# A new order of instructions at the start and at the end of a fused attention and mixture kernel, and half a weight unit loaded early

## The chip, the cores and the metric

The kernel runs on one core of a Trainium2 chip. The metric is the device time of one execution in microseconds (us). The core has five engines with a queue of instructions each: TensorE (PE in the rows; its weight loads are PEld), VectorE (DVE), ScalarE (ACT), GpSimd (POOL) and SyncE (SP), which in this kernel issues all transfers. An engine works through its own queue strictly in order; between engines, semaphores hold an instruction back until its inputs are there and the buffer that it writes is free.

## What is computed

Three layers follow one another on 4608 rows of 512 numbers:

```python
# attention without a score matrix: 8 batches, 8 heads, 576 positions, 64 wide
q_s = softmax(q, over the 64);  k_s = softmax(k, over the 576 positions)
x   = q_s @ (k_s.T @ v)                       # per batch and head -> x [4608, 512]
# feed-forward with a cosine gate (w_in, w_out are given as float64)
h = x @ w_in;  g = h * cos(h);  x2 = g @ w_out          # 2048 wide, back to 512
# soft mixture: 32 slots, 8 experts of 4 slots each
logits = x2 @ phi;  d = softmax(logits, over rows);  c = softmax(logits, over slots)
slot_in = d.T @ x2;  slot_out[e] = relu(slot_in[e] @ w1[e]) @ w2[e]
out = c @ slot_out
```

## The kernel before

The rows are worked in nine blocks of 512. The last block is cut into two parts of 256, so there are ten parts. A part has 16 steps, one for each 128 of the 2048 columns of `w_in`; the kernel numbers the steps through, from 0 to 159, and the last 32 have half the width.

One step is this chain. TensorE makes `h` for 128 columns by 12 matmuls (`mm1`, L906): x and `w_in` are each split into a high and a low part, and three products are summed. The result stands in one of three PSUM buffers ("h"). `round_u` (L925) rounds it to a whole number of turns, on ScalarE or VectorE as a table says; `frac` (L934, VectorE) takes the fraction; `cosine` (L940, ScalarE) looks up a sine; `gate` (L943, VectorE) multiplies and writes `g` into the big buffer G. The gate frees the PSUM buffer, so `mm1` of step s waits for the gate of step s-3. Every two or four steps `logits` (L946) adds those steps to the slot logits, in the PSUM bank LT, and `g_tr` (L963, VectorE) transposes their `g` in place. After the 16 steps of a part come the softmax sums: `p1` copies the logits out of PSUM, `p2` transposes them for the combine weights (`c1` to `c3`), `p3` takes the running maximum, `p4` the exponentials, `p5`, `copies` and `take_copy` spread them out, `g_mm` (L1099) adds d.T @ g to four PSUM banks, and `g_add` (L1114) moves these into an accumulator.

The rounded number and the fraction stand in a tile T of four places of 512 (`tbuf`, L357); step s uses place s modulo 4.

The start is special. Before step 0 the first block's x is made: `k_max`, `k_sub`, `k_exp` (the softmax of k), `k_v` (k_s.T @ v on TensorE), `k_fin`, `q_max` to `q_mul` (the softmax of q), `q_tr` and `q_tr_ev` (transposes and their copies), `q_kv` (TensorE), and the split of x by `x_hi` (ScalarE) and `x_lo` (VectorE). At the same time the float64 weights arrive in eight chunks each of `w_in` and `w_out` and are turned into float32 by VectorE, ScalarE and GpSimd (`convert`, L763, three instructions a piece; `conv_wi` parts 3 and 4, L805, split a piece into high and low). The `w_out` pieces are written back to DRAM for the end, and with phi they are folded into one matrix for the logits (`w2_tr`, `w2_tr_ev`, `w2_mm`, `w2_sum`). Step f needs piece f of `w_in`, so steps 0 to 15 run while pieces still arrive; blocks 1 and 2 are prepared in the same time. `warm` matmuls (L1691) compute nothing: they fill TensorE while it waits.

The end is special too. After step 159 follow the sums of the last part, `fold`, `gT`, `si` (the slot inputs, with `w_out`), `siT`, and the experts: `w1` (16 matmul groups), `hs`, `hT`, `w2` (17 groups), `so`, `sx`, and then `om` and `oe`, which multiply and copy out nine blocks, and `out`, which stores them. The experts' weights are 32 MB. They come in units of 1 MB through SyncE's queue (`load_unit`, L1188), each into a buffer that the earlier work no longer needs (`slots`, L1164); `units_after` (L1746) says what each waits for. Unit 20, the first of `w2`, goes to T, and waits for the last gate.

What sets the order: one list of work items is written out by the kernel. `PLACES["AT"]` gives every item a number, items are issued in the order of their numbers, and each engine's queue is that list cut down to the engine. `PLACES["ENG"]` gives the engine of items that can go to two or three (D is VectorE, A ScalarE, P GpSimd).

Of the kernel before, what the change touches and what calls it, by code (L numbers as in the profile page):

```python
# [17 lines left out]
AX = mybir.AxisListType  # L18
# [10 lines left out]
                "warm": [95, 30, 116, 83, 20, 16, 26, 18, 63, 10, 138, 33, 40, 120, 27, 2, 12, 6,  # L29
# [5 lines left out]
                "k_max": [17, 19, 21, 23, 25, 29, 32, 39, 173, 177, 195, 222, 178, 223, 229, 236,  # L35
# [3 lines left out]
        "k_tr": [44, 242],  # L39
        "k_dg": [46, 50, 247, 262],  # L40
        "k_bc": [53, 280],
        "k_bc_ev": [65, 281, 528, 642, 834, 949, 1107, 1272],
                "k_sub": [66, 88, 96, 69, 323, 338, 326, 335, 542, 541, 529, 531, 654, 648, 661,
            643, 837, 861, 841, 844, 970, 951, 958, 950, 1125, 1121, 1111, 1116, 1281, 1285, 1274,
            1278],
                "k_exp": [75, 93, 101, 77, 356, 347, 543, 532, 662, 672, 869, 875, 992, 1001, 1151,
            1166, 1306, 1313],
                "k_v": [102, 107, 362, 363, 556, 558, 679, 684, 885, 888, 1013, 1019, 1188, 1193,
            1358, 1365],
        "k_fin": [115, 381, 574, 697, 895, 1028, 1205, 1375],  # L50
# [232 lines left out]
def attention_cosine_moe_softmoe(  # L283
# [35 lines left out]
    def misc():  # L319
        return pst("m", 4)  # L320
# [1555 lines left out]
```

## Time and profile before

| | us |
|---|---|
| three timed runs, median (lowest, highest) | 656.82 (655.79, 657.02) |
| the profiled execution's own time | 659.79 |
| its span, from the first to the last instruction | 657.8 |
| TensorE busy in the span | 625.2 (95%) |
| VectorE busy | 536.6 (82%) |
| ScalarE busy | 366.3 (56%) |
| GpSimd busy | 128.4 (20%) |
| first big matmul of step 0 | 33.36 |
| last part's `g_mm` ends, near | 583.2 |

The span is the profiled execution's; its own time stands 2.0 us over the span, and 3.0 us over the median of the timed runs. A row of the timeline is read so: start, length, engine, line, operation, what it writes and reads, how many were merged into the row, and in square brackets how long the engine had been idle before and what ended that.

### The profile page before, as it was taken

What the parts mean: (1) busy time and instruction counts of PE and PEld (TensorE: products, weight loads), DVE (VectorE), ACT (ScalarE), POOL (GpSimd) and SP (SyncE); (2) the same over time, 40 slices, a digit from 0 to 9 for tenths busy, and PEclk for the clock granted to TensorE, in tenths of its full rate; (3) what the DMA queues carried; (4) which work ended last, traced back from release to release, by engine and by line L of the source; (5) the groups of instructions that cost most, each with busy time, mean ns of one, the idle gap of its engine ahead of it and who ended that gap; (6) DMA issues with size and microseconds to landing.
All of it is one profiled execution on the core that took longest, in us unless ns stands there. A gap on an engine that the chain in (4) does not pass through costs nothing.

```text
span 657.8 us, 18204 instructions
## 1 busy us (share of the span) xinstructions
PE 625.2 (95%) x7745; PEld 474.6 (72%) x7745; DVE 536.6 (82%) x1075; ACT 366.3 (56%) x642; POOL 128.4 (20%) x131
## 2 busy tenths in 40 slices
PE   5899999999999999999999999999999999999990
PEld 4577777688868877877788788778878989843440
DVE  7889999999999988998979987879988878842251
ACT  4789988657475476457466542635536456530051
POOL 4343535243133043041220120001200000000000
PEclk9889999999999999999999999999999999999996
DMA  9997965354321442133302300021003338899968
GB/s 314 301 398 246 341 222 145 115 154 129 87 53 34 121 114 82 49 101 112 80 18 80 125 0 2 1 77 54 1 1 124 135 111 308 323 372 422 386 233 347
DMA packets 60992, 103.88 MB, mean 158 GB/s; under 512 B 9456, under 2 KB 40560, under 8 KB 55920
## 3 DMA queue, kind: packets, MB, share of 16 engines
q1 hardware_dynamic: 60912, 102.74, 46.4%
q8 instruction: 60, 0.98, 0.6%
q14 instruction: 20, 0.16, 0.1%
HBM read 88.15 MB, written 14.57 MB: 156 GB/s over the span
## 4 chain that ended last, share of the span: by engine, by line
PE 74%; DMA 9%; ACT 7%; DVE 6%; issue 1%; POOL 1%; SPq 0%; DVEq 0%; POOLq 0%; ACTq 0%
PE ps_h L920 53%; PE ps_m L1107 6%; PE ps_LT L958 5%; DMA w_u<-in_moe_w_dram 3%; PE ps_m L708 2%; PE ps_m L523 2%; DMA Q<-in_q_dram 2%; DMA out_dram<-ob 1%; DMA G<-in_moe_w_out_dram 1%; PE ps_h L1312 1%; DMA wo<-G 1%; ACT T L928 1%; ACT T L941 1%; PE ps_LT L1696 1%; ACT G L775 1%
## 5 line engine op out<-in xcount | busy, mean ns | idle before, releaser
L920 PE MATMUL ps_h<-XH,W 128*128 128x512 f32 x1024 | 328.7, 396 | 0.9 <-DVE G L944 0.9
L920 PEld LDWEIGHTS ps_h<-XH,W 128*128 128x128 f32 x1024 | 193.3, 189 | 53.5 <-issue 8.1
L920 PE MATMUL ps_h<-XL,W 128*128 128x512 f32 x512 | 200.5, 392 | 0.0
L941 ACT ACTIVATE T<-T 128x512 f32<-128x512 f32 (+1 forms) x160 | 92.6, 587 | 93.8 <-DVE T L936 93.5
L928 ACT ACTIVATE T<-ps_h,quarter 128x512 int32<-128x512 f32 (+1 forms) x123 | 79.4, 646 | 80.1 <-PE ps_h L920 79.2
L944 DVE TENSOR_TENSOR G<-T,ps_h 128x512 f32<-128x512 f32 (+1 forms) x160 | 99.4, 624 | 25.0 <-ACT T L941 19.6
L920 PEld LDWEIGHTS ps_h<-XL,W 128*128 128x128 f32 x512 | 96.8, 189 | 18.8
L936 DVE SCALAR_TENSOR_TENSOR T<-T,ps_h 128x512 f32<-128x512 int32 (+1 forms) x160 | 99.0, 623 | 10.2 <-ACT T L928 8.9
L965 DVE STREAM_TRANSPOSE G<-G 128x512 f32<-128x512 f32 (+1 forms) x160 | 98.4, 637 | 0.3 <-PE ps_LT L958 0.2
L420 POOL TENSOR_TENSOR Q<-Q,qm 128x512 f32<-128x512 f32 x33 | 35.2, 1083 | 150.3 <-DVE qm L417 104.6
L920 PE MATMUL ps_h<-xe,W 128*128 128x256 f32 x384 | 48.0, 285 | 0.0
L920 PEld LDWEIGHTS ps_h<-xe,W 128*128 128x128 f32 x384 | 46.6, 192 | 1.6 <-DVE G L944 0.8
L684 POOL TENSOR_TENSOR KVB<-KVB,km 128x576 f32<-128x576 f32 x22 | 33.1, 1526 | 72.9 <-DVE km L677 50.6
L441 POOL TENSOR_TENSOR Q<-Q,qm 128x512 f32<-128x512 f32 x27 | 27.9, 1060 | 81.6 <-DVE qm L434 64.1
L958 PE MATMUL ps_LT<-G,wphi 128*32 128x128 f32 (+1 forms) x1280 | 38.9, 265 | 1.0 <-issue 1.0
L958 PEld LDWEIGHTS ps_LT<-G,wphi 128*32 128x32 f32 x1280 | 30.3, 110 | 9.3 <-issue 6.6
L1107 PE MATMUL ps_m<-G,A 32*32 32x512 f32 x1024 | 35.7, 598 | 0.0
L941 ACT ACT_TABLE_LOAD x24 | 30.8, 1283 | 0.4
L930 DVE TENSOR_SCALAR T<-ps_h 128x512 int32<-128x512 f32 (+1 forms) x37 | 22.8, 615 | 7.0 <-PE ps_h L920 7.0
L1107 PEld LDWEIGHTS ps_m<-G,A 32*32 32x32 f32 x1024 | 16.9, 103 | 13.4 <-issue 7.9
L417 DVE TENSOR_REDUCE qm<-Q 128x8 f32<-128x512 f32 x36 | 24.1, 673 | 2.7 <-DMA Q<-in_q_dram 2.7
L1125 DVE SCALAR_TENSOR_TENSOR gacc<-gacc,ac,ps_m 128x512 f32<-128x512 f32 x32 | 23.2, 733 | 2.3 <-PE ps_m L1107 2.3
(214 smaller groups left out, 716.9 us busy)
## 6 DMA issues: line engine op xcount, KB each, us to landing
w_u<-in_moe_w_dram SPq DMA_DIRECT2D x22, 1024.0 KB, 8.0
KVB<-in_k_dram SPq DMA_DIRECT2D x16, 576.0 KB, 5.2
KVB<-in_v_dram SPq DMA_DIRECT2D x32, 256.0 KB, 4.4
out_dram<-ob SPq DMA_DIRECT2D x8, 1024.0 KB, 9.1
rwi<-in_moe_w_in_dram SPq DMA_DIRECT2D x7, 1024.0 KB, 10.2
G<-in_moe_w_dram SPq DMA_DIRECT2D x7, 1024.0 KB, 7.8
rwo<-in_moe_w_out_dram SPq DMA_DIRECT2D x5, 1024.0 KB, 11.0
wo<-G SPq DMA_DIRECT2D x16, 256.0 KB, 6.0
```

Of the source, the lines that this page charges most:

```text
L417: nc.vector.reduce_max(out=qm[:, t], in_=qv(t), axis=AX.X)
L420: (nc.vector if eng == "DVE" else nc.gpsimd).tensor_tensor(out=qv(t), in0=qv(t), in1=qm[:, t].unsqueeze(2).to_broadcast([128, 8, 64]), op= ...
L441: (nc.vector if eng == "DVE" else nc.gpsimd).tensor_tensor(out=qv(t), in0=qv(t), in1=qs[:, t].unsqueeze(2).to_broadcast([128, 8, 64]), op= ...
L684: (nc.vector if eng == "DVE" else nc.gpsimd).tensor_tensor(out=k_t[:, t], in0=k_t[:, t], in1=km[:, t].unsqueeze(1).to_broadcast([128, KC, ...
L920: nc.tensor.matmul(out=u_t[s], lhsT=w[:, wi, kk, o:o + 128], rhs=x[xi][:, kk], start=(kk == 0 and n == 0), stop=(kk == 3 and n == 2),)
L928: nc.scalar.activation(out=t.bitcast(I32), in_=u_t[s], func=ACTF.Identity, bias=quarter)
L936: nc.vector.scalar_tensor_tensor(out=t, in0=t.bitcast(I32), scalar=0.25, in1=u_t[s], op0=ALU.subtract, op1=ALU.subtract)
L941: nc.scalar.activation(out=t_t[s], in_=t_t[s], func=ACTF.Sin, scale=-UNDER_TWO_PI)
L944: nc.vector.tensor_tensor(out=g_of(s), in0=t_t.pop(s), in1=u_t.pop(s), op=ALU.mult)
L958: nc.tensor.matmul(out=lt_t[d][32 * c:32 * c + 32, 0:w], lhsT=w2sb[:, f], rhs=g[:, w * c:w * c + w], start=(f0 == 0), stop=(f0 == NF - 1),)
L965: nc.vector.transpose(out=g_of(s), in_=g_of(s))
L1107: nc.tensor.matmul(out=st["gp"][i][32 * c:32 * c + 32].rearrange("p (f b) -> p f b", f=NF) if d < NB else st["gp"][i][32 * c:32 * c + 32]. ...
```

## The change

1. The numbers in `AT` are new for the items up to about step 20 (and those issued among them) and for those after step 127. Between them the list is the same, item for item. SyncE's queue has the same transfers in the same order, with one more (point 3), which stands between units 5 and 6.
2. 24 letters of `ENG` change up to step 40. Net of exchanges they move three `k_sub` from VectorE to GpSimd; `cD` (the low part of a `w_in` piece) of pieces 1, 5, 7 and 8 from VectorE to GpSimd and of piece 15 the other way; one `q_mul` from GpSimd to VectorE; three `w2_tr_ev` and four `round_u` from ScalarE to VectorE. In the last two parts four more `round_u` change, from VectorE to ScalarE.
3. T becomes two tiles, T and T2, of two places each. The last two parts use T alone (four places of 256). T2 is free after the gates of steps 126 and 127, and half of unit 20 is loaded into it then (`load_half`); the other half still goes to T, after the last gate.
4. In the last two parts one `g_tr` transposes two steps' `g` (512 columns) in place of two instructions of 256.
5. The logits of the last two parts: `p2` and `c1` to `c3` of both are issued after `si`; `p3` and `p4` of the last part read the logits from PSUM and no longer wait for the copy of `p1`. The `fill` matmuls (they compute nothing) stand elsewhere.

```diff
-        "k_sub": "DDDPPDDDPPDPPPPPPPDPPPPDPPPPPPDP",
+        "k_sub": "DPDDDPPPPPPPPPPPPPDPPPPDPPPPPPDP",
-        "cD": "DDPPPDPDDPPPPPPP",
+        "cD": "DPPPPPPPPPPPPPPD",
...
-        t = t_t[s] = tbuf[:, s % 4, 0:parts[s // NF][2]]
+        if s < 16 * (NB - 1):
+            t = t_t[s] = tb[s % 4 // 2][:, s % 2]
+        else:
+            t = t_t[s] = tb[0][:, s % 4 // 2, 256 * (s % 2):256 * (s % 2) + 256]
...
+        if d >= NB - 1:
+            f = tile_of(d, f)
+            x = gs(d)[:, f:f + 2] if d < NB else gs(d)[:, f // 8, f % 8:f % 8 + 2]
+            x = x.rearrange("p a t -> p (a t)")
+        nc.vector.transpose(out=x, in_=x)
...
-        nc.vector.reduce_max(out=es, in_=st["lt"], axis=AX.X)
+        nc.vector.reduce_max(out=es, in_=lt_of(d), axis=AX.X)
...
+    def lt_of(d):
+        return st["lt", d] if d < NB else lt_t[d][:, 0:parts[d][2] // 4]
...
+    def load_half():
+        ut["T2"] = sbt([128, 2, 512], "T2", name="w2_h")
+        nc.sync.dma_start(out=ut["T2"], in_=w2_src(units[slots.index("T")])[:, 2:4])
...
+            if slots[i] == "T":
+                ut[un], src = (t, ut.pop("T2")), src[:, 0:2]
...
+    op(("half",), DMA, 1.3, load_half, more=2.3, slack=1.4, after=[("g", S8 - 1), ("g", S8 - 2)])
```

VectorE at the start, before: from the reciprocal of the first q sums (L434) to the first sum of `k_fin` (L716). L684 is `k_sub`, L448 `q_mul`, L800 the join of a converted piece, L815 `cD`.

```order
L434 RECIPROCAL qm<-qm 128x32
L800 SCALAR_TENSOR_TENSOR G<-G,rwo 128x512
L448 TENSOR_TENSOR B<-Q,qm 128x8x64 x2
L800 SCALAR_TENSOR_TENSOR A<-A,rwi 128x512
L684 TENSOR_TENSOR KVB<-KVB,km_76 128x576
L800 SCALAR_TENSOR_TENSOR A<-A,rwi 128x512
L684 TENSOR_TENSOR KVB<-KVB,km_76 128x576
L815 TENSOR_TENSOR W_228<-A,W_228 128x4x128
L448 TENSOR_TENSOR B<-Q,qm 128x8x64
L815 TENSOR_TENSOR W_228<-A,W_228 128x4x128
L417 TENSOR_REDUCE qm<-Q 128x8
L716 TENSOR_REDUCE rs<-ps_m 128x2 x2
```

The same stretch now:

```order
L434 RECIPROCAL qm<-qm 128x32
L684 TENSOR_TENSOR KVB<-KVB,km_77 128x576
L448 TENSOR_TENSOR B<-Q,qm 128x8x64 x2
L684 TENSOR_TENSOR KVB<-KVB,km_77 128x576 x2
L800 SCALAR_TENSOR_TENSOR A<-A,rwi 128x512
L448 TENSOR_TENSOR B<-Q,qm 128x8x64 x2
L815 TENSOR_TENSOR W_266<-A,W_266 128x4x128
L716 TENSOR_REDUCE rs<-ps_m 128x2 x2
```

The subtractions for k now stand ahead of all conversions, and two conversions (one L800, one L815) have left the stretch.

ScalarE before, from the last two parts of x (L593) to the first sine (L941); L928 is the rounding of a step, L427 the exponentials of q, and L775 with A a new `w_in` piece.

```order
L593 CAST XH_97<-ps_m 128x512 x2
L775 ACTIVATE G<-rwo 128x512 x2
L813 CAST W_358<-A 128x4x128
L786 ACTIVATE rwo<-rwo,low 128x512
L928 ACTIVATE T<-ps_h,quarter 128x512
L427 ACTIVATE Q<-Q 128x512 x4
L849 COPY cst<-ps_m 128x4x128
L928 ACTIVATE T<-ps_h,quarter 128x512
L775 ACTIVATE A<-rwi 128x512
L941 ACT_TABLE_LOAD
L941 ACTIVATE T<-T 128x512
```

The same stretch now (L931 is the rounding, L944 the sine):

```order
L593 CAST XH_98<-ps_m 128x512 x2
L786 ACTIVATE rwo<-rwo,low 128x512
L775 ACTIVATE G<-rwo 128x512
L849 COPY cst<-ps_m 128x4x128
L786 ACTIVATE rwo<-rwo,low 128x512
L849 COPY cst<-ps_m 128x4x128
L813 CAST W_367<-A 128x4x128
L775 ACTIVATE G<-rwo 128x512
L427 ACTIVATE Q<-Q 128x512 x4
L931 ACTIVATE T<-ps_h,quarter 128x512
L775 ACTIVATE A<-rwi 128x512
L944 ACT_TABLE_LOAD
```

The exponentials of q stand ahead of the first rounding, and the second rounding has gone to VectorE; the new `w_in` piece still stands ahead of the table load for the first sine.

TensorE at the end, before, from the last `g_mm` (L1107) on; L1696 are fill matmuls, L1239 and L1250 `fold`, L1266 `gT`, L1282 `si`, L1298 `siT`.

```order
L1107 MATMUL ps_m<-G,KVB_u 32x512 x32
L1696 MATMUL ps_LT<-ones 128x512
L1239 MATMUL ps_h<-gacc,rf 32x256 x8
L1250 MATMUL ps_h<-G,rf 32x2x64 x16
L1266 MATMUL ps_m<-ident,gacc 128x128 x4
L1696 MATMUL ps_LT<-ones 128x512 x2
L1282 MATMUL ps_m<-KVB_u,gT 32x512 x4
L1696 MATMUL ps_LT<-ones 128x512 x2
L1077 MATMUL ps_h<-esacc,rr 128x1
L1282 MATMUL ps_m<-KVB_u,gT 32x512 x4
L1696 MATMUL ps_LT<-ones 128x512
L1282 MATMUL ps_m<-wo_u,gT 32x512 x8
```

The same stretch now (L1125 is `g_mm`, L1725 fill, L1266 and L1277 `fold`, L1293 `gT`, L1309 `si`, L1008 `p2`):

```order
L1125 MATMUL ps_m<-G,KVB_u 32x512 x32
L1725 MATMUL ps_LT<-ones 128x512
L1266 MATMUL ps_h<-gacc,rf 32x256 x8
L1277 MATMUL ps_h<-G,rf 32x2x64 x16
L1725 MATMUL ps_LT<-ones 128x512
L1293 MATMUL ps_m<-ident,gacc 128x128 x4
L1725 MATMUL ps_LT<-ones 128x512
L1095 MATMUL ps_h<-esacc,rr 128x1
L1309 MATMUL ps_m<-KVB_u,gT 32x512 x8
L1309 MATMUL ps_m<-wo_u,gT 32x512 x8
L1008 MATMUL ps_m<-ident,late 64x64 x4
```

The four `si` now follow one another; the three fills that stood between them are gone, and the small matmul for the sum (L1077, now L1095) stands ahead of them.

## Rows read from the trace of the kernel before

**Rows 1.** Windows by stage: per engine busy us (instructions), granted clock, DMA share, GB/s.

```profile
33.30:38.50 5.20, 5.20 (x16) 4.07 (x14) 4.39 (x8) 3.40 (x7) 0.66 (x1) 0.56 1.04 396
...
60.00:90.00 30.00, 29.70 (x356) 23.57 (x354) 29.65 (x56) 29.41 (x51) 12.74 (x11) 1.00 0.95 310
...
120.00:574.00 454.00, 451.76 (x5642) 364.65 (x5641) 400.89 (x809) 249.34 (x429) 74.17 (x72) 1.00 0.30 91
...
627.00:658.00 31.00, 14.43 (x330) 6.12 (x326) 12.31 (x22) 10.38 (x22) 0.00 (x0) 0.80 0.76 306
```

**Rows 2.** Timeline of TensorE: first k_v, and the first matmul of step 0.

```profile
21.41 2.33 PE L708 MATMUL ps_m<-KVB 64*64 64x66 f32 x144
...
33.36 0.80 PE L920 MATMUL ps_h<-XH,W 128*128 128x512 f32 x1
```

**Rows 3.** Timeline of VectorE, ScalarE and GpSimd, 32 to 46 us.

```profile
32.15 0.69 DVE L417 TENSOR_REDUCE qm<-Q 128x8 f32<-128x512 f32 x1 [1.65 <-DMA Q<-in_q_dram]
...
38.48 0.69 ACT L928 ACTIVATE T<-ps_h,quarter 128x512 int32<-128x512 f32 x1 [1.64 <-PE ps_h L920]
...
39.44 0.66 POOL L790 TENSOR_SCALAR rwi<-rwi 128x512 int32<-128x512 uint16 x1 [5.49 <-DMA rwi<-in_moe_w_in_dram]
...
42.20 0.67 ACT L775 ACTIVATE A<-rwi 128x512 f32<-128x512 f32 x1
...
42.89 1.28 ACT L941 ACT_TABLE_LOAD   x1
...
44.19 0.63 ACT L941 ACTIVATE T<-T 128x512 f32<-128x512 f32 x1
...
44.85 0.69 DVE L944 TENSOR_TENSOR G<-T,ps_h 128x512 f32<-128x512 f32 x1 [0.37 <-ACT T L941]
```

**Rows 4.** Timeline of GpSimd and VectorE: `cD` on either, and two that overlap.

```profile
40.19 1.31 POOL L815 TENSOR_TENSOR W<-A,W 128x512 fp32r<-128x512 f32 x1
...
55.11 1.27 POOL L448 TENSOR_TENSOR B<-Q,qm 128x512 f32<-128x512 f32 x1 [0.86 <-DVE qm L434]
55.40 1.53 DVE L800 SCALAR_TENSOR_TENSOR G<-G,rwo 128x512 int32<-128x512 int32 x1
...
59.70 0.68 DVE L815 TENSOR_TENSOR W<-A,W 128x512 fp32r<-128x512 f32 x1
```

**Rows 5.** Windows, the end of the steps and the expert weights.

```profile
500.00:536.00 36.00, 36.00 (x553) 30.96 (x562) 31.37 (x71) 22.59 (x43) 0.00 (x0) 1.00 0.32 119
...
584.00:590.00 6.00, 5.73 (x71) 2.90 (x63) 1.63 (x5) 0.85 (x3) 0.00 (x0) 1.00 0.97 326
590.00:619.00 29.00, 28.79 (x332) 11.85 (x335) 7.42 (x11) 1.52 (x3) 0.00 (x0) 1.00 1.01 418
```

**Rows 6.** Timeline of SyncE: the issue of units 21 and 22.

```profile
583.31 2.94 SPq L1208 DMA_DIRECT2D G<-in_moe_w_dram  x2
```

**Rows 7.** The chain that ended last: its wait for the expert weights.

```profile
606.08 17.84 DMA w_u<-in_moe_w_dram
```

**Rows 8.** Timeline of VectorE around the last gate (L944; L965 are transposes).

```profile
575.96 0.38 DVE L944 TENSOR_TENSOR G<-T,ps_h 128x256 f32<-128x256 f32 x1
576.26 1.73 DVE L965 STREAM_TRANSPOSE G<-G 128x256 f32<-128x256 f32 x5
...
579.25 1.40 DVE L965 STREAM_TRANSPOSE G<-G 128x256 f32<-128x256 f32 x4
```

**Rows 9.** Groups by shape, 495 to 580 us: busy us, mean ns; idle.

```profile
L965 DVE STREAM_TRANSPOSE G<-G 128x512 f32<-128x512 f32 x14 | 9.5, 693 | 0.2 <-PE ps_LT L958 0.2
```

**Rows 10.** Timeline of TensorE: last `g_mm`, and fills and `si` after it.

```profile
580.85 2.35 PE L1107 MATMUL ps_m<-G,KVB_u 32*32 32x512 f32 x64
...
587.88 0.73 PE L1696 MATMUL ps_LT<-ones 128*128 128x512 f32 x2
...
589.65 0.50 PE L1696 MATMUL ps_LT<-ones 128*128 128x512 f32 x1
590.08 1.92 PE L1282 MATMUL ps_m<-wo_u,gT 128*32 128x512 f32 x16
```

More of the change, by code (lines that the diff above doesn't have):

```diff
@@ L41 @@
-        "k_bc": [53, 280],
-        "k_bc_ev": [65, 281, 528, 642, 834, 949, 1107, 1272],
-                "k_sub": [66, 88, 96, 69, 323, 338, 326, 335, 542, 541, 529, 531, 654, 648, 661,
+                "k_max": [1, 6, 7, 11, 8, 14, 16, 22, 166, 174, 179, 225, 162, 170, 176, 180, 451,
[3 rows of a table added]
+        "k_tr": [30, 230],
+        "k_dg": [36, 40, 248, 254],
+        "k_bc": [43, 274],
+        "k_bc_ev": [44, 290, 508, 642, 834, 949, 1107, 1272],
+                "k_sub": [61, 59, 69, 78, 317, 319, 335, 334, 520, 516, 527, 539, 654, 648, 661,
@@ L222 @@
+        "gT": [2075, 2076],
+        "gTe": [2080, 2082],
+        "si": [2081, 2084, 2085, 2087],
+        "siT": [2095, 2096, 2099],
[14 rows of a table added]
+        "out": [2201, 2210, 2216, 2225, 2232, 2243, 2255, 2256],
+        "half": [1792],
     },
     "ENG": {
-        "k_sub": "DDDPPDDDPPDPPPPPPPDPPPPDPPPPPPDP",
+        "k_sub": "DPDDDPPPPPPPPPPPPPDPPPPDPPPPPPDP",
         "q_sub": "PDPPPPPDPPPPPPPPPPPPPPPPPPPPPPPPPDPP",
-        "q_mul": "DDDPDPPPPPPPPPPPPPPPPPDPPPPPPPPPPPPP",
+        "q_mul": "DDDDPPPDPPPPPPPPPPPPPPDPPPPPPPPPPPPP",
@@ L356, in attention_cosine_moe_softmoe @@
     bbuf = sbt([128, 4, 512], "B")
-    tbuf = sbt([128, 4, 512], "T")
+    tb = [sbt([128, 2, 512], tag) for tag in ("T", "T2")]
     kv_t = [abuf[:, 0, 256 * i:256 * i + 256].rearrange("p (h t d) -> p h t d", h=2, t=2)
@@ L978, in p1 @@
     def p1(d):
-        st["lt"] = sbt([128, 128], "LTs")[:, 0:parts[d][2] // 4]
-        nc.scalar.copy(out=st["lt"], in_=lt_t.pop(d)[:, 0:parts[d][2] // 4])
+        w = parts[d][2] // 4
+        if d < NB - 1:
+            st["lt", d] = sbt([128, 128], "LTs")
+        elif d == NB - 1:
+            late = sbt([128, 128], "phi", name="late")
+            st["lt", d], st["lt", d + 1] = late[:, 0:w], late[:, w:2 * w]
+        nc.scalar.copy(out=st["lt", d], in_=lt_t[d][:, 0:w])
+    def lt_of(d):
+        return st["lt", d] if d < NB else lt_t[d][:, 0:parts[d][2] // 4]
     def p2(d):
-        pm = st["t"] = misc()
+        pm = st["t", d] = misc()
         if d < 8:
-            nc.tensor.matmul(out=pm[:, 0:128], lhsT=st["lt"], rhs=ident, start=True, stop=True)
+            nc.tensor.matmul(out=pm[:, 0:128], lhsT=st["lt", d], rhs=ident, start=True, stop=True)
             return
@@ L991, in p2 @@
                 out=pm[64 * h:64 * h + 64, 0:64].rearrange("p (e s) -> p e s", e=2),
-                lhsT=st["lt"], rhs=cols[:, h], start=True, stop=True,
+                lhsT=st["lt", d], rhs=cols[:, h], start=True, stop=True,
             )
     def p3(d):
-        nc.vector.reduce_max(out=es, in_=st["lt"], axis=AX.X)
+        nc.vector.reduce_max(out=es, in_=lt_of(d), axis=AX.X)
         if d == 0:
@@ L1351, in e_w2 @@
             return
+        w = ut["w2", eg, u]
         for x in range(2):
             for q4 in range(4):
+                wq = w[q4 // 2][:, q4 % 2] if isinstance(w, tuple) else w[:, q4]
                 nc.tensor.matmul(
@@ L1643, in step_ops @@
                + [past("warm", i) for i in range(NWARM)] * (d == 0 and f == n - 1))
-            for i in range(s - n + 1, s + 1):
-                op(("tr", i), DVE, cost(0.05, 0.56), g_tr, i, after=[("tl", s)])
+            for i in range(s - n + 1, s + 1, 1 if nt == 512 else 2):
+                op(("tr", i), DVE, 0.61, g_tr, i, after=[("tl", s)])
     def tls(d):
@@ L1655, in post_ops @@
         op(("p1", d), ACT, 0.25 if big else 0.2, p1, d,
-           after=[("tl", 16 * d + 15), past("p2", d - 1), past("p4", d - 1)])
+           after=[("tl", 16 * d + 15), past("p2", d - 1) if d < NB - 1 else None, past("p4", d - 1)])
         op(("p2", d), PE, 0.15 if big else 0.25, p2, d, take="m", after=[("p1", d)])
@@ L1659, in post_ops @@
         op(("p3", d), DVE, 0.42 if big else 0.36, p3, d,
-           after=[("p1", d), past("p6", d - 1), past("p4", d - 1)])
+           after=[("p1", d) if d < NB else ("tl", 16 * d + 15), past("p6", d - 1), past("p4", d - 1)])
         op(("p4", d), ACT, (0.6 if d else 0.35) if big else 0.5, p4, d, table="exp",
@@ L1675, in post_ops @@
                + each("tc", d)
-               + ([("tr", 16 * d + i) for i in range(NF)] if jq == 0 else []))
+               + ([("tr", 16 * d + i) for i in range(0, NF, 1 if big else 2)] if jq == 0 else []))
         for i in range(4):
@@ L1762, in lus @@
     def lus(*kind):
-        return [("lu", i) for i, u in enumerate(units) if u in kind]
+        return [("lu", i) for i, u in enumerate(units) if u in kind] + [("half",)] * (
+            units[slots.index("T")] in kind
+        )
+    op(("half",), DMA, 1.3, load_half, more=2.3, slack=1.4, after=[("g", S8 - 1), ("g", S8 - 2)])
     unit_ops(0, 23)
@@ L1769, in attention_cosine_moe_softmoe @@
     for i in range(NFILL):
-        op(("fill", i), PE, 0.26, keep_warm, 1, at=FILL, after=[("p1", D)])
+        op(("fill", i), PE, 0.26, keep_warm, 1, at=FILL, after=[("p1", D), ("p4", D)])
     for x in range(2):
```

104 lines of the change are left out of this document (49 added, 55 removed), and 162 rows, old and new, of the table PLACES.

## Prediction

> **What bounds the kernel now.** I read the windows by stage first, to see which engine has no room in which stretch. From 120 to 574 us TensorE is busy 451.8 of 454 us at full clock: what is won or lost ahead of that stretch goes through it unchanged, since one list of work runs there without gaps. From 60 to 90 us TensorE has 29.70 of 30 us, but VectorE 29.65 and ScalarE 29.41 too, so three engines bound this stretch at once and GpSimd, with 12.74 us, is the only one with room. From 33.3 to 38.5 us TensorE works at a granted clock of 0.56, the lower level. From 627 us on TensorE has 14.4 of 31 us; the chain of small products, multiplications and stores there is not touched by the change, so it is a tail of fixed length [rows 1].
>
> Then I read the timelines of single engines at the two places where the list is new. At the start, the reader is to see what the first gates wait for: step 0's matmuls begin at 33.36 [rows 2], its rounding at 38.48, its gate only at 44.85 [rows 3]. At the end, the windows and the chain that ended last show that not TensorE but the transfer of the expert weights decides: 418 GB/s and a DMA share of 1.01 from 590 to 619 us [rows 5], and 17.84 us of the chain from 606.08 on are a wait for a transfer [rows 7]. So the time is the start's delay, plus a dense middle, plus the arrival of the last weight unit, plus the tail. The change acts on the first and the third.
>
> **The start.** Step 0's gate, which frees the first of three PSUM buffers, is at the end of a chain on ScalarE: a new `w_in` piece (42.20, 0.67 us), the load of the sine table (42.89, 1.28), the sine (44.19, 0.63), then on VectorE the gate (44.85, 0.69), done at 45.54 [rows 3]. From the start of the first to the end of the last are 3.34 us. The transfer that brings that piece had landed at 39.44, when GpSimd's part of it began [rows 3]; between 39.17, where step 0's rounding ends, and 42.20 ScalarE worked off four exponentials of q, a copy and the rounding of step 1, as the order shows. In the new order the exponentials stand ahead of step 0's rounding, one copy stands earlier and the rounding of step 1 has gone to VectorE. So the piece can begin when it lands, at 39.44, and the gate ends at 39.44 + 3.34 = 42.78 instead of 45.54: 2.76 us earlier. Step 3 waits for that gate.
>
> This holds if steps 0 to 2 are through by then. Before step 0's last matmuls stood the low part of x on VectorE, and ahead of it now the maximum of q that waits for its transfer until 32.15 and takes 0.69 us [rows 3]. With about 0.7 us for the low part and 0.8 for a matmul at the low clock (the first took that [rows 2]), step 0 ends near 34.3 instead of just under 38.48: up to 4.2 us, which is the far end of the gain. The near end: if TensorE, with fewer warm matmuls ahead, works one more step at 0.56, that costs 5.20 x (1 - 0.56) = 2.3 us [rows 1], and the 2.76 shrinks to 0.5; a second such step would make it a loss of 1.8. I take -2.5: nearly the whole 2.76, since the gate hangs on a landing and on ScalarE's own order, with 0.26 off for what follows.
>
> What follows is steps 3 to 40. Net, six pieces of work leave VectorE (three `k_sub`, three `cD`, each near the 0.68 us of a `cD` [rows 4]) and eight come (four roundings, three `w2_tr_ev`, one `q_mul`): (8 - 6) x 0.68 = 1.4 us more. ScalarE gives up seven, some 4.8 us at the 0.69 of a rounding [rows 3]. GpSimd takes six and gives one: a `cD` lasts 1.31 us there [rows 4], so 5 x 1.31 = 6.6 us, in an engine that is idle more than half of 60 to 90 [rows 1]. ScalarE's relief is worth something only where it, and not VectorE, ended a wait; VectorE's 1.4 us are hidden only where it is not full. The bounds for this part are +1.4, all of it on the path, and -0.7, one rounding less in front of the steps' sines; I take +0.26, near nothing, because four of the six subtractions and conversions that move stand ahead of step 0, where VectorE still waits for transfers (1.65 us before 32.15 alone [rows 3]).
>
> **The end of the steps.** In the last two parts an instruction on 512 columns takes 693 ns [rows 9] and two on 256 take 2 x 0.346 = 0.69 (1.73 for five [rows 8]): the joined transposes save nothing by themselves. They stand otherwise among the gates, so the last gate (ended 576.34 [rows 8]) may come 0.35 to 0.7 us later, and half a unit's transfer with it. After it, `p3` no longer waits for a copy, and the transposes that followed (four, 1.40 us, from 579.25 [rows 8]) are spread; I put the last `g_mm`, which began its final run at 580.85 [rows 10], at 0.2 us earlier.
>
> Half of unit 20, 0.524 MB, leaves the full stretch: at 418 GB/s that is 1.25 us [rows 5]. It is loaded from about 517 us on instead, in a stretch where the DMA share is 0.32 [rows 5]; there it costs nothing. Behind it the queue has a second loss: units 21 and 22 were issued at 583.31 only, when G is free [rows 6], and from 584 to 590 the transfers moved 326 GB/s instead of 418, that is 6 x 92 = 0.55 MB or 1.3 us too little [rows 5]. If the shorter unit 20 is through before unit 21 is issued, the 1.25 us turn into a longer pause and the gain is only the 0.2 us by which `g_mm` ends earlier; if the queue stays full, 1.25 us and up to the 1.3 us of the pause come back, -2.6 together. Both ends rest on rows of this stretch; I take -1.4, the 1.25 and the 0.2, because a share of 0.97 at 584 to 590 says that the queue still had packets under way.
>
> After `g_mm` three groups of fills that stood between the `si` (0.73 and 0.50 us are two of them, [rows 10]) leave the path, some 1.7 us of TensorE. That is not added: `w1` waits for the units anyway [rows 7]. If that cover were gone, it would count.
>
> **The sum.** -2.5 - 1.4 = -3.9. The profiled execution has a span of 657.8 and its own time is 659.79; these become 653.9 and 655.9. The median of the runs shown, 656.82, is 3.0 below that own time, so I forecast 655.9 - 3.0 = 652.9.
>
> **Rival 1: the lead is spent on VectorE.** All 1.4 us of VectorE's extra work fall on the path, one block by GpSimd of 0.85 us (below) is added, and the start is left with -2.5 + 1.4 + 0.85 = -0.25. With half of the half unit's gain, -0.6, the sum is -0.85: 656.0. For it: 29.65 of 30 [rows 1]. Against it: a lead of TensorE is lost only once, and ScalarE gains 4.8 us in the same stretch.
>
> **Rival 2, slower: GpSimd's new work holds VectorE up.** One `k_sub` or `cD` reads two operands from SBUF. When a GpSimd multiplication ran from 55.11 to 56.38, a VectorE join that began at 55.40 lasted 1.53 us, where a like instruction takes 0.68 [rows 4]: 0.85 us lost, and its end came 0.55 after GpSimd's. Five more such instructions on GpSimd, at 0.85 to a whole 1.31 us each and 1.08 in the middle, are 5.4 us in a stretch where VectorE has no reserve: -3.9 + 5.4 = +1.5, that is 658.3. It cancels the gain from 3.9 us of stalls on and is measurably slower from 5.2. Against it: some of the five stand ahead of step 0, and VectorE may be waiting where they run.
>
> The Trainium skill ("SBUF — State Buffer", Who interferes with whom) has the rule behind this rival: VectorE's second pair of ports is shared with GpSimd, and of a VectorE instruction with two SBUF inputs and a GpSimd instruction that reads SBUF the one that starts second is wholly blocked until the first ends. The row agrees within 0.13 us: 56.38 + 0.68 is 57.06, and the join ended at 56.93. By that rule each of the five costs VectorE up to its whole length where the two meet; by the reading that they only slow each other, less.
>
> **Rival 3: the half unit buys nothing.** Unit 21 stays tied to the end of `g_mm`; the end gives -0.2, the start -2.5: 654.1. For it: the issue at 583.31 right behind the last `g_mm` [rows 6, 10]. Against it: the share of 0.97.
>
> That the change does not do what it says is a rival in the start: if the pieces of `w_in` and q land later because the transfers themselves slip, nothing has reserve, since the maximum of q and the `w_in` piece stand in order ahead of everything; a slip would pass on one to one. It is inside rival 1's time.
>
> **Chances.** The forecast 0.50, rival 1 0.22, rival 3 0.14, rival 2 0.14. About 0.2%, 1.3 us, is what a measurement of this kernel can tell from no change. The forecast and rival 3 are faster, and a part of rival 1, 0.07: faster 0.71. The other 0.15 of rival 1 is within: same 0.15. Rival 2: slower 0.14. The forecast's own range is 651 to 655, from a full -1.25 - 1.3 at the end to one without it. The low end with the far start (-4.2) and the far end (-2.6) would be 650.0; I stop at 650.2. The high end, 657.6, takes in rival 1 and the near half of rival 2.
>
> **What would show it.** Step 0's gate should end near 42.8 and the `w_in` piece before the table load begin at 39.4, not later. The last gate of the steps should come 2 to 3 us earlier than 576.34. Unit 21 should be issued near 580.6, and the gap in the transfers behind it be smaller. The last wait for `w1` should end some 3.9 us earlier, and the tail from there stay at 31 us. The forecast is wrong if TensorE's granted clock in steps 0 to 2 stays low for a second step, if VectorE has several conversions of 1.3 us or more beside GpSimd's, or if the pause behind unit 20 grows by as much as the unit shrank.

## The result, and the profile after

The changed kernel takes 650.61 us (median of 4, 650.04 to 651.63) against 656.52 for the kernel before; the ratio is 0.9917, 95% interval 0.9895 to 0.9938. Measured again later (experiment 12) it is 0.9915, 0.9890 to 0.9940. That is 5.5 us of 656.6 (0.0083 x 656.6; the two medians differ by 5.9); forecast were 3.9, and 652.9 us.

Two executions have to be compared with care. The one behind [rows 1 to 10] took 659.79 us, 3.3 over its median. Experiment 1 took a second profile of the kernel before, with a span of 653.3 instead of 657.8. What differs is a transfer. Each transfer comes in sixteen parts; the table has the times at which the first, the fifteenth and the last part landed, the start of step 3, the end of the last step, and how long after it TensorE's last w2 group began and the last weight unit landed (worked out from the traces; us).

```
                    w_out chunk 1          w_in chunk 2           step 3  last step  w2     unit
before [rows]       26.06  30.15  31.07    34.85  38.53  39.37    46.01   574.33     52.17  52.13
before again        26.30  28.05  28.34    34.60  35.92  37.14    41.82   570.26     51.53  51.49
changed             26.20  27.39  28.99    34.56  36.11  36.46    39.95   565.61     51.39  50.16
changed again       26.29  27.78  29.29    34.71  36.30  36.61    40.09   566.11     51.39  50.92
start only (exp. 2) 26.18  27.59  29.22    34.63  36.34  36.52    39.99   566.76     52.16  52.12
end only (exp. 3)   26.38  27.94  28.48    34.49  36.09  36.27    41.50   569.97     51.39  50.75
no half (exp. 4)    26.32  27.91  29.21    34.68  36.53  36.60    40.08   565.74     51.71  51.66
```

In the first profile two parts of one chunk came 4 to 5 us after the first, and the landings behind them in the table and at w_in chunk 3 (48.54, against 46.35 in the second profile) were 2 to 3 us late; in none of the other thirteen profiles did a part of that chunk come 4 us late (at most 3.6). So the like-for-like gain at step 3 is 41.82 - 39.95 = 1.9 us, not the 6.1 that the two first profiles show, and at the end of the steps 570.26 - 565.61 = 4.7.

Windows of the changed kernel (us, then busy time and count of PE, PEld, DVE, ACT, POOL, granted clock, DMA share, GB/s):

```profile
12.40:17.50 5.10, 4.08 (x14) 2.96 (x12) 5.03 (x11) 4.33 (x9) 2.12 (x2) 1.00 1.17 319
17.50:21.00 3.50, 3.16 (x128) 2.88 (x131) 3.28 (x7) 3.50 (x7) 0.00 (x0) 1.00 1.08 348
...
33.30:38.50 5.20, 5.20 (x29) 3.72 (x29) 5.13 (x12) 4.31 (x7) 1.88 (x2) 1.00 1.04 405
...
60.00:90.00 30.00, 29.01 (x362) 23.10 (x361) 28.27 (x56) 27.85 (x49) 18.12 (x15) 1.00 0.93 299
...
584.00:590.00 6.00, 6.00 (x51) 1.58 (x45) 2.47 (x13) 0.52 (x2) 0.00 (x0) 1.00 1.01 423
590.00:619.00 29.00, 28.95 (x360) 12.91 (x352) 5.84 (x5) 1.90 (x4) 0.00 (x0) 1.00 0.83 342
```

The same view of the kernel before, second profile:

```profile
12.40:17.50 5.10, 0.92 (x4) 0.40 (x3) 5.03 (x9) 4.74 (x10) 2.17 (x2) 0.94 1.17 315
17.50:21.00 3.50, 2.85 (x11) 2.59 (x12) 3.50 (x7) 2.87 (x6) 0.00 (x0) 0.50 1.08 346
21.00:24.00 3.00, 3.00 (x81) 2.48 (x83) 3.00 (x6) 2.96 (x6) 1.62 (x1) 0.55 1.03 217
...
60.00:90.00 30.00, 29.42 (x380) 22.37 (x379) 29.87 (x56) 29.94 (x54) 15.98 (x14) 1.00 0.95 307
```

Before, TensorE worked 0.92 of 5.10 us from 12.4 to 17.5 and then had the lower clock until 24 us (the record has 0.5 from 16.86 to 23.69). Now twelve of the warm matmuls stand there (37 in all, as before; 20 of them began ahead of 9 us, now 8 do), and from 14.71 us on the clock is full, from 33.3 to 38.5 too, where the first profile had 0.56. One thing about this column has to be known: the changed kernel's trace has no record of the clock before 14.71 us, and where there is none the view prints 1.00. The matmuls tell what the clock was: those of 512 columns that follow one another begin 0.43 us apart until 14.70 and 0.23 apart from there on, so before 14.71 the lower of the two levels held.

At the end the window of 584 to 590 is full (423 GB/s); the pause now lies ahead of it, from 579 to 583. From 590 to 619 the transfers' share is 0.83, since the last unit has landed at 615.77, and TensorE waits for no unit there. From 60 to 90 VectorE and ScalarE are busy 1.6 and 2.1 us less ([rows 1] had 29.65 and 29.41). Of the timelines, first the changed kernel: `k_v`, the maximum of q, the `w_in` piece, table load, sine and first gate:

```profile
19.17 2.41 PE L708 MATMUL ps_m<-KVB 64*64 64x66 f32 x144 [0.21 <-ACT rwi L786]
...
30.08 0.69 DVE L417 TENSOR_REDUCE qm<-Q 128x8 f32<-128x512 f32 x1 [0.79 <-DMA Q<-in_q_dram]
...
36.55 0.68 ACT L775 ACTIVATE A<-rwi 128x512 f32<-128x512 f32 x1 [0.87 <-DMA rwi<-in_moe_w_in_dram]
37.24 1.28 ACT L944 ACT_TABLE_LOAD   x1
38.54 0.63 ACT L944 ACTIVATE T<-T 128x512 f32<-128x512 f32 x1
...
39.20 0.69 DVE L947 TENSOR_TENSOR G<-T,ps_h 128x512 f32<-128x512 f32 x1
```

The kernel before, second profile (answers to [rows 2 to 4]); ScalarE's rows from the rounding of step 0 to the `w_in` piece follow one another without a gap:

```profile
22.18 3.01 PE L708 MATMUL ps_m<-KVB 64*64 64x66 f32 x144
...
34.65 0.67 ACT L928 ACTIVATE T<-ps_h,quarter 128x512 int32<-128x512 f32 x1
35.22 2.18 ACT L427 ACTIVATE Q<-Q 128x512 f32<-128x512 f32 x4
37.31 0.57 ACT L849 COPY cst<-ps_m 128x512 f32<-128x512 f32 x1
37.77 0.69 ACT L928 ACTIVATE T<-ps_h,quarter 128x512 int32<-128x512 f32 x1
38.35 0.67 ACT L775 ACTIVATE A<-rwi 128x512 f32<-128x512 f32 x1
...
41.01 0.69 DVE L944 TENSOR_TENSOR G<-T,ps_h 128x512 f32<-128x512 f32 x1 [1.00 <-ACT T L941]
...
51.27 1.27 POOL L448 TENSOR_TENSOR B<-Q,qm 128x512 f32<-128x512 f32 x1 [0.88 <-DVE qm L434]
51.55 1.53 DVE L800 SCALAR_TENSOR_TENSOR G<-G,rwo 128x512 int32<-128x512 int32 x1
...
67.51 1.60 DVE L684 TENSOR_TENSOR KVB<-KVB,km 128x576 f32<-128x576 f32 x1
```

The first gate ends at 39.89 instead of 41.70. The rows of 51.55 and 67.51 are VectorE instructions that lasted 0.85 us too long beside GpSimd. Counting those that exceed the median of their kind by over 0.25 us up to 120 us, there are five with 3.9 us in excess (2.7 of them behind the start of step 3); in the changed kernel there are two, the join at 38.11 (1.02 us) and the one at 58.62 (1.12), 0.8 us together (0.4 behind the start of step 3). The chain that ended last now goes through the start as follows (start, length, what): a transfer of q, the maximum that waits for it, the low part of x behind it, and then TensorE without a break.

```profile
22.22 7.77 DMA Q<-in_q_dram
...
30.08 0.69 DVE qm L417
30.76 0.61 DVE XL L603
31.37 0.04 issue
31.42 6.20 PE ps_h L920 x26
```

### The profile page after: what moved, and what is told of

The parts are those of the page before. It is cut to its first block, busy times and chain, and to the rows that moved or that the text cites. A ratio compares the mean times of both kernels' runs of the same rounds, so it can differ in the third digit from the quotient of the medians.

```text
span 648.3 us, 18189 instructions
## 1 busy us (share of the span) xinstructions
PE 620.8 (96%) x7745; PEld 472.0 (73%) x7745; DVE 531.5 (82%) x1057; ACT 364.1 (56%) x639; POOL 134.6 (21%) x136
## 4 chain that ended last, share of the span: by engine, by line
PE 87%; DMA 5%; DVE 3%; SPq 1%; issue 1%; POOL 1%; ACT 0%; DVEq 0%; POOLq 0%; ACTq 0%
PE ps_h L920 60%; PE ps_m L1125 6%; PE ps_LT L961 5%; PE ps_m L708 3%; PE ps_m L523 2%; PE ps_m L1383 2%; DMA out_dram<-ob 1%; PE ps_LT L1725 1%; DMA Q<-in_q_dram 1%; PE ps_h L1339 1%; DMA rwi<-in_moe_w_in_dram 1%; PE ps_m L1339 1%; PE ps_m L844 1%; SPq L383 1%; DVE G L974 1%
## 5 line engine op out<-in xcount | busy, mean ns | idle before, releaser
L944 ACT ACTIVATE T<-T 128x512 f32<-128x512 f32 (+1 forms) x160 | 92.8, 587 | 91.1 <-DVE T L939 90.7
L931 ACT ACTIVATE T<-ps_h,quarter 128x512 int32<-128x512 f32 (+1 forms) x123 | 78.4, 640 | 82.7 <-PE ps_h L920 81.1
L974 DVE STREAM_TRANSPOSE G<-G 128x512 f32<-128x512 f32 x144 | 96.6, 691 | 0.2 <-PE ps_LT L961 0.2
L684 POOL TENSOR_TENSOR KVB<-KVB,km 128x576 f32<-128x576 f32 x25 | 37.8, 1538 | 71.2 <-DVE km L677 28.8
L1125 PE MATMUL ps_m<-G,A 32*32 32x512 f32 x1024 | 35.7, 598 | 0.0
L1125 PEld LDWEIGHTS ps_m<-G,A 32*32 32x32 f32 x1024 | 16.9, 103 | 13.4 <-issue 7.9
L1725 PE MATMUL ps_LT<-ones 128*128 128x512 f32 x59 | 24.1, 508 | 1.7 <-DVE r L342 1.7
```

The costliest lines, as they stand in the source:

```text
L684: (nc.vector if eng == "DVE" else nc.gpsimd).tensor_tensor(out=k_t[:, t], in0=k_t[:, t], in1=km[:, t].unsqueeze(1).to_broadcast([128, KC, ...
L931: nc.scalar.activation(out=t.bitcast(I32), in_=u_t[s], func=ACTF.Identity, bias=quarter)
L944: nc.scalar.activation(out=t_t[s], in_=t_t[s], func=ACTF.Sin, scale=-UNDER_TWO_PI)
L974: nc.vector.transpose(out=x, in_=x)
L1125: nc.tensor.matmul(out=st["gp"][i][32 * c:32 * c + 32].rearrange("p (f b) -> p f b", f=NF) if d < NB else st["gp"][i][32 * c:32 * c + 32]. ...
L1725: nc.tensor.matmul(out=warm[when], lhsT=ones_r, rhs=ones_r.unsqueeze(1).to_broadcast([128, 4, 128]), start=True, stop=True,)
```

## The experiments

All ratios are to the kernel before, run on the same chip, five rounds each, 95% intervals in brackets.

**1. The kernel before, unchanged.** 

> The kernel before, unchanged, to see how much of its profiled execution was chance: that execution took 659.79 us against a median of 656.5, and in it TensorE's granted clock was 0.5 to 0.6 from 31 to 37.5 us and one of the sixteen parts of the w_out piece that landed at 31.07 came 4.5 us behind the other fifteen. If both are chance, this profile has a span near 655, step 0 ends before 37 us and the last gate near 573.5; if they belong to the order of the work, the span is 657 to 658 again and the first gate ends near 45.5. Ratio 1.000 within 0.2%.

Ratio 0.9999 [0.9984, 1.0014], span 653.3. Both oddities of the first profile were chance. The forecast's lengths of work hold, but where it reads a time off a landing, that is 2 to 3 us late.

**2. The start alone.** Edit: the old kernel with the new numbers for the first 596 items and the 24 letters. 

> The kernel before with only the new order and letters up to step 20 and step 40 (596 items, the 24 letters); end as before, no half unit. Theory: the start carries most of the change, because transfers get out earlier and TensorE keeps its clock; 5 us of the 5.9 are here, 651.5. Rival: the half unit and the end carry half of it, then 653.5 to 654. Second rival (the forecast's -2.5): 654.0.

0.9942 [0.9924, 0.9959]: 3.8 us, most of the gain. The median, 652.46, lies between the theory's 651.5 and the rivals' 653.5 to 654.

**3. The end alone.** Edit: the changed kernel with the old numbers and letters for the start. 

> The changed kernel with the old order and letters up to step 20 and 40; the new end with the half unit stays. Theory: after the new end TensorE, no longer the last weight unit, is late, so only some 0.8 us are gained: 655.7. Rival: the whole gain of the transfers' side arrives, -2.0 to -2.6: 654.2.

0.9990 [0.9975, 1.0004]: 0.7 us, near the theory's 0.8 but not told apart from nothing. Both halves alone give 4.5 of the 5.5; the difference is no larger than the intervals.

**4. No half unit early.**

```diff
-        nc.sync.dma_start(out=ut["T2"], in_=w2_src(units[slots.index("T")])[:, 2:4])
...
-                ut[un], src = (t, ut.pop("T2")), src[:, 0:2]
+                ut[un] = (t, ut.pop("T2"))
+                nc.sync.dma_start(out=ut[un][1], in_=src[:, 2:4])
+                src = src[:, 0:2]
```

> The changed kernel, but both halves of unit 20 are loaded after the last gate. Theory: the last unit lands 1.2 us later, at 617.0 in the place of 615.8, and TensorE's last w2 group began at 617.0 anyway; cost 0 to 0.3, 650.6 to 650.9. Rival (the half unit is worth its transfer, 1.25 us): 651.9.

0.9929 [0.9913, 0.9944]: 0.8 us more than the changed kernel, with overlapping intervals. The last unit lands 51.7 us after the last step instead of 50.2 to 50.9, but the last w2 group begins only 0.3 later (51.71). The half unit moves the transfers by about its 1.25 us; a third of that or less reaches TensorE in the trace. The time, 651.61, lies between the theory (650.6 to 650.9) and the rival (651.9) and decides for neither.

**5. SyncE's queue late at 46 us.**

```diff
+PLACES["AT"]["oW"][7] = 288.05
+PLACES["AT"]["lv"][5] = 288.2
+PLACES["AT"]["oW"][4] = 288.3
+PLACES["AT"]["lwi"][6] = 288.4
+PLACES["AT"]["oW"][6] = 288.5
```

> The changed kernel, but in SyncE's queue a v piece, the write-back of w_out piece 4 and w_in chunk 6 stand behind the write-back of w_out piece 7, which waits for VectorE's join of that piece (56.05 us in the changed kernel). Nothing else moves. Chunk 6 should land near 65 instead of 60.3, as it did in the kernel before (63.6 and 67.5). Theory A: the gain between step 3 and step 24 (1.2 us more than at step 3) comes from transfers that no longer wait in this queue; then 1 to 1.5 us are lost, 651.6 to 652.1. Rival B: it comes from the work's new spread over the engines, and the transfers have reserve; then within 0.3, 650.6.

1.0012 [0.9999, 1.0024]: the whole gain is gone, over four times what theory A expected. Steps run as in the changed kernel up to step 9 (65.9 against 65.7), then waits come one behind the other (from 64 to 90 us, engine, line waited for, us, times, longest):

```profile
POOL G L795 <- DMA G<-in_moe_w_out_dram: 7.5, 1, 7.5
...
ACT G L780 <- DMA G<-in_moe_w_out_dram: 3.4, 1, 3.4
...
PE ps_m L713 <- DVE cst L854: 2.2, 1, 2.2
PE ps_h L925 <- POOL W L820: 2.0, 1, 2.0
```

The `w_out` chunk lands at 77.26 instead of 70.80; GpSimd's instruction for it stands in order ahead of the low part of a `w_in` piece, which step 11 needs. After that wait of TensorE the clock falls:

```profile
78.00:80.00 2.00, 0.42 (x1) 0.40 (x2) 0.41 (x1) 0.44 (x1) 1.84 (x2) 0.93 1.06 343
80.00:82.00 2.00, 2.00 (x6) 1.54 (x5) 1.11 (x3) 2.00 (x5) 0.30 (x1) 0.50 1.05 320
```

So in this list the transfers have no reserve for a delay of this size: chunk 6 of `w_in` landed at 66.56 instead of 60.29, the `w_out` chunk 6.5 us late. That does not show that they made the old list slow; experiment 11 asks that.

**6. The old letters of `k_sub` and `cD`.** 

> The changed kernel with the old letters of k_sub and cD: the six pieces of work that went from VectorE to GpSimd go back. Forecast's rival 2 (GpSimd's work blocks VectorE): faster, by up to 0.85 us for each, at least 1 us, 649.5. Theory: VectorE is full there and gets 6 x 0.68 = 4 us more, of which some 1 to 2 end on the path: 651.6 to 652.6.

1.0067 [1.0045, 1.0090], 661.1 us: 10 us slower than the changed kernel. Rival 2 is refuted as it stood, and the loss is far over the theory's. VectorE's instructions beside GpSimd are now nine with 6.3 us in excess, though GpSimd does less. How much of the 10 us that is, the run does not tell.

**7. The old letters of the rounding and `w2_tr_ev`.** 

> The changed kernel with the old letters of the rounding and of w2_tr_ev up to step 40: net seven pieces go back from VectorE to ScalarE. Theory: ScalarE's relief is what the steps 3 to 24 gained by; then about 1 to 1.5 us slower, 651.6 to 652.1. Rival (VectorE's 1.4 us are the cost, as the forecast's rival 1 had it): faster, by up to 1 us, 649.6 to 650.6.

1.0015 [0.9999, 1.0031]: 6.4 us slower than the changed kernel; the theory's direction, over four times its size. Up to step 9 it is 0.8 late; then TensorE stops within `k_v` of block 1, for nothing that the profile's waits show, and has the lower clock afterwards (timeline of TensorE):

```profile
69.50 2.41 PE L828 MATMUL ps_m<-KVB 64*64 64x66 f32 x130
75.22 0.46 PE L828 MATMUL ps_m<-KVB 64*64 64x65 f32 x14 [3.31 <-issue]
```

Windows of it:

```profile
76.00:78.00 2.00, 2.00 (x9) 1.68 (x9) 1.93 (x7) 0.58 (x2) 0.00 (x0) 0.72 0.50 82
78.00:80.00 2.00, 2.00 (x6) 1.52 (x5) 1.72 (x4) 0.00 (x0) 0.00 (x0) 0.50 1.01 397
```

Step 10 begins 3.4 us and step 11 5.0 us later than in the changed kernel, of 7.1 us at the end of step 127: most of the loss in this trace arises at the stop and in the lower clock behind it, and the run does not tell what the letters cost by themselves.

The changed kernel stops in the same place for 1.0 us. What ends such stops can be read from the trace's transfers: in the fourteen profiles there are 27 of 0.4 us or more between 30 and 580 us that have no releaser, and each ends 1.2 to 1.6 us after a 16 KB transfer of the queue of instructions (q8) has landed. Here that transfer lands at 73.97, in the changed kernel at 70.55 (its stop ends at 71.79). So TensorE seems to have waited for its next instructions; no run moves such a transfer by itself, and why it is 3.4 us late here is open.

**8. Fewer fills between w1 and w2.** Edit: `PLACES["AT"]["fill"][7]` to `[17]` = 100000, which leaves them out. 

> The changed kernel without eleven of the fill matmuls that stand between the groups of w1 and w2 (they compute nothing). Theory: in the changed kernel TensorE, and no longer the last weight unit, is late at the end: the unit lands at 615.8 and its group begins at 617.0; without the fills TensorE waits for the unit, and 1.2 us are gained: 649.4. Rival: the granted clock falls when TensorE waits there, or the transfer was last all the time: 650.6 or more.

0.9916 [0.9889, 0.9943], as the changed kernel. In the trace TensorE now does wait for units, and its last w2 group begins 49.7 us after the last step instead of 51.4; the span is 647.3:

```profile
PE ps_m L1394 <- DMA w_u<-in_moe_w_dram: 2.7, 2, 1.4
```

That in the changed kernel the fills, not the last unit, set when that group begins is shown by the trace; that their loss is worth time is not shown by the timed runs.

**9. ScalarE's old order at the first gate.**

```diff
+PLACES["AT"]["q_exp"][4] = 182.5
+PLACES["AT"]["v"][1] = 182.7
```

and step 1's letter of `v` back to A. 

> The changed kernel with ScalarE's order at the first gate put back: the exponentials of q (2.2 us) behind step 0's rounding, and step 1's rounding on ScalarE again, ahead of the w_in piece. The forecast's reason for the start: that order held the piece back, so the first gate (ends 39.89) comes about 2 us later and 1.5 to 2 us are lost, 652.5. Rival: since step 0 ends at 32.2, ScalarE gets through both before the piece lands at 36.46 (it begins at 36.55); the landing sets the gate, within 0.4 us, 650.6 to 651.0.

0.9918 [0.9890, 0.9947], 650.77: nothing is lost. ScalarE's timeline:

```profile
32.87 0.70 ACT L934 ACTIVATE T<-ps_h,quarter 128x512 int32<-128x512 f32 x1
33.45 2.20 ACT L430 ACTIVATE Q<-Q 128x512 f32<-128x512 f32 x4
35.53 0.70 ACT L934 ACTIVATE T<-ps_h,quarter 128x512 int32<-128x512 f32 x1
36.47 0.68 ACT L778 ACTIVATE A<-rwi 128x512 f32<-128x512 f32 x1 [0.25 <-DMA rwi<-in_moe_w_in_dram]
```

The rounding of step 0 begins at 32.87, where it began at 34.65 in the kernel before, so ScalarE is through with all of it before the piece lands. The new order of this queue is not needed for the gain. That does not show that the queue was no hindrance in the old order; the part on the forecast comes back to it.

**10. Without twelve warm matmuls.** Edit: warm 1, 8, 11, 12, 14, 19, 24 to 27, 29 and 35 left out. 

> The changed kernel without the twelve warm matmuls that fill TensorE from 12.4 to 16.5 us (they compute nothing). TensorE is then idle there for 4 to 5 us as it was before, and the granted clock should fall to 0.5 near 17.6 to 21. Theory A: the early clock is part of the start's gain; k_v ends 1 us later and step 0 too, and 0.5 to 1.5 us reach the end, 651.5. Rival B: the landing at 36.46 sets the first gate anyway; within 0.4, 650.6.

0.9979 [0.9963, 0.9996]: 655.7, so 4.2 us (0.0064 x 656.6) of the 5.5 are lost. Windows:

```profile
12.40:17.50 5.10, 0.00 (x0) 0.00 (x0) 5.03 (x11) 4.34 (x9) 2.15 (x2) 1.00 1.17 318
17.50:21.00 3.50, 3.49 (x52) 3.05 (x56) 3.32 (x6) 3.50 (x8) 0.00 (x0) 1.00 1.09 348
```

Timelines of TensorE and VectorE:

```profile
19.84 3.90 PE L720 MATMUL ps_m<-KVB 64*64 64x66 f32 x144
...
23.78 0.23 DVE L728 TENSOR_REDUCE rs<-ps_m 128x2 f32<-128x4 f32 x2 [2.31 <-PE ps_m L720]
```

The 1.00 in both windows is no measurement: the record of the clock begins at 23.28 in this trace. Before it two matmuls of 512 columns begin 0.43 us apart (9.49 and 9.92), behind it 0.23. So after 5.1 us without work the 144 matmuls of `k_v` run at the lower clock for most of their time, take 3.90 us instead of 2.41 and end at 23.74 instead of 21.58. VectorE waits 2.31 us for them and is full from there on, so the first gate ends at 42.13 instead of 39.89 and step 3 begins 2.2 later. By step 26 it is 3.8: 0.8 more come at 73 to 75 us, where TensorE waits 2.1 us for `k_fin` of block 1 and the changed kernel has its stop of 1.0, and 1.1 between steps 24 and 26, where a stop of 0.75 us (it ends at 147.31) follows an instruction transfer that landed at 146.03.

**11. Chunk 6 early in the kernel before.**

```diff
+PLACES["AT"]["lv"][5] = 217.2
+PLACES["AT"]["lwi"][6] = 217.4
```

> The kernel before with one edit: in SyncE's queue a v piece and w_in chunk 6 stand ahead of the write-back of w_out piece 5, which VectorE's late join holds for 7.6 to 9.3 us. Chunk 6 lands 4 us earlier (near 59.5 instead of 63.6). Theory A (the transfers' gap alone made steps 3 to 24 slower before): 1 to 2 us faster than before, ratio 0.997 to 0.9985. Rival B (before's order of work uses the chunk no earlier): 1.000 within 0.1%.

1.0013 [0.9993, 1.0034]: rival B. Chunk 6 landed at 59.44 instead of 63.62 (experiment 1), and nothing was won: the gap in the old queue cost the old list nothing.

**12. The changed kernel again.** 

> The changed kernel, unchanged, beside the three others on the same chip, and for a second profile: ratio 0.9917 as at first, 650.6, span 648 to 649; the unit landing last near 615.8 and TensorE's last w2 group 1 us behind it.

0.9915 [0.9890, 0.9940], span 649.2. The last unit is half a microsecond ahead of the last w2 group here, not one.

## Why the forecast was right, and where it was not

The direction was right. The measured 650.61 lies within the whole range, 650.2 to 657.6, but near its end: the forecast called 651 to 655 its own part of it, and that was missed by 0.4. By its own steps:

- **Step 0 and the gate.** Both lengths hold within 0.1 us. Step 0 ends 2.2 us after the landing of q on which the maximum waits: 29.98 and 32.16 in the changed kernel, 32.05 and 34.3 in the forecast; a little luck is in it, since 0.8 stood for one matmul at the lower clock, and two at the full clock took 0.74. The gate ends 3.34 us after the `w_in` piece begins (36.55, 39.89), and the piece begins as it lands. But the landings read from [rows 3] were 2 to 3 us late by chance, and so was the gate of before: the gain at step 3 is 1.9, not 2.76.
- **The reason was half right.** The forecast had the piece freed from ScalarE's queue. In the old order it does stand there: landed at 37.14, 36.27 and 37.08 in experiments 1, 3 and 11, it begins at 38.35, 37.98 and 38.22, right behind the rounding of step 1. These 1.1 to 1.7 us are most of the 1.4 to 1.8 by which it begins earlier in the changed kernel (36.55). But the new order of that queue is not what the gain needs: with the old one put back nothing is lost (experiment 9), because step 0 ends at 32.1 instead of 34.3 and ScalarE is through early enough for both. Whether the new order of the queue would do alone, with step 0 where it was, no run tests.
- **What the forecast left out is the clock at `k_v`.** In the new order `k_v` starts at 19.17 and runs at the full rate (2.41 us). Without the twelve warm matmuls it still starts at 19.84, but is slow, and step 3 begins no earlier than before (42.18 against 41.82): 4.2 us go (experiment 10). In the old order its rate mattered little: with `k_v` at 20.43 for 2.33 us (experiment 3) step 3 begins at 41.50, with 22.18 and 3.01 (experiment 1) at 41.82; ScalarE's queue stood behind it in both. The forecast named the warm matmuls only as a danger, with TensorE slower in the new order; in [rows 2] the old `k_v` had lasted 2.33 us, and nothing there showed that its rate was at stake.
- **The step that failed in size is "what follows" the gate, steps 3 to 40.** It was put at +0.26 with bounds of +1.4 and -0.7. Between step 3 and step 24 the lead grows from 1.9 to 3.1 us (138.59 to 135.48), so the term is -1.2, outside its bounds. It counted VectorE's instructions (+1.4 us) and not how long they last: up to step 24 there are two more, but VectorE is busy 125.3 us instead of 126.6, and its excess beside GpSimd fell from 3.9 to 0.8 us. That this is where the 1.2 us come from is argued, not shown: ScalarE too is busy 2.7 us less from step 3 to step 24 (78.2 for 80.9), and no experiment changes either alone. The gate gave 0.9 less than forecast and this term 1.5 more, so the two errors offset each other in part.
- **The middle was not quite unchanged.** From step 24 to the end of step 127, where the lists are alike, the lead grows from 3.1 to 4.1. Part of this is chance: between the start alone (experiment 2) and the changed kernel, alike up to there, the same stretch differs by 0.5.
- **Rival 2 had the mechanism and the wrong sign.** GpSimd holds VectorE up, but five pieces more on GpSimd came with fewer meetings, and the old letters in the new order with more (experiment 6: 6.3 us). The rule of the Trainium skill ("SBUF — State Buffer", Who interferes with whom), that the instruction which starts second is blocked, agrees again: the GpSimd row of 51.27 ends at 52.54, and the join's end at 53.08 is 0.54 later, near the 0.68 that a join takes. All seven VectorE instructions counted above, five before and two now, end 0.54 to 0.62 us after a GpSimd instruction that ran beside them. So it matters which pairs meet, not only how many instructions an engine has.
- **Rival 1** (VectorE carries 1.4 us more) did not come: VectorE is busy 1.6 us less in 60 to 90, and 1.3 less up to step 24.
- **The end.** Forecast -1.4. The pause of [rows 5 and 6] moved and did not go away: in the changed kernel units 20 and 21 land at 576.70 and 579.20, 2.5 apart, and unit 22 4.2 later (583.36), where before the 4.1 stood between units 20 and 21 (586.95, 591.06). So of the far bound the 1.3 us of the pause did not come back in this profile, and the 1.25 of the half unit did on the side of the transfers. The last unit lands 50.2 to 50.9 us after the last step instead of 51.3 to 52.1. But the cover that the forecast named is gone: the last w2 group now waits for TensorE's own queue, fills among it, at 51.39 in three profiles of the new end, against 51.39 to 52.17 in four of the old one. Alone the end gives 0.7 (experiment 3), above the start 1.6 (0.9942 to 0.9917). Another 0.6 us, not foreseen, come in the last blocks, from the end of step 127 to that of step 159: the four matmuls of `p2` (0.35 us) no longer stand there; the rest is open.
- **The sum** was -3.9; measured are -5.5: -3.8 for the start where -2.5 stood, and the end between -0.7 and -1.6 where -1.4 stood.

Open: why the instruction transfer of experiment 7 is late, whether ScalarE's new queue would do alone, what the meetings of VectorE and GpSimd cost by themselves, and whether the fills cost time. The losses of experiments 5, 6, 7 and 10 (6.2, 10, 6.4 and 4.2 us) are together far more than 5.5: they show what the new order needs, not how the gain divides.

## What to carry to other kernels

Before a time is read off a transfer's landing, take a second profile: two late parts of one transfer moved the landings behind it by 2 to 3 us. Ask of each engine that is full not only how many instructions it gains, but what runs beside them. And where a full engine waits for TensorE, look at what TensorE did in the microseconds before: leaving twelve matmuls that compute nothing out of the new order cost 4.2 us, where the whole change had brought 5.5.

## What the runs showed of the hardware

A granted clock of 1.00 can stand for no record. In experiment 10 the windows say 1.00 from 12.4 to 21 us, but the record begins at 23.28, and `k_v` takes 3.90 us there instead of 2.41; in the changed kernel it begins at 14.71. In both, matmuls of 512 columns begin 0.43 us apart before that time and 0.23 behind it. So the distance of equal matmuls has to be read beside the clock's column.

TensorE's stops without a releaser, 0.4 to 3.3 us long, ended 1.2 to 1.6 us after a 16 KB instruction transfer had landed, in all 27 cases of the fourteen profiles: they look like waits for instructions.

And an order of work this tight falls as a whole: putting two tables of letters back, or moving five transfers, cost 6 to 10 us where the whole change had brought 5.5.
